# Storing a transposed gradient by column groups, loading it in four transfers, and another order of the last four rows

## The chip, the cores and the metric

The kernel runs on one core of a Trainium2 chip. The core has a tensor engine (PE, with its weight loads shown apart as PEld), a vector engine (DVE), a scalar engine (ACT), GpSimd (POOL) and a sync engine (SP). Transfers are carried by 16 DMA engines, which SP, ACT and POOL feed through queues of their own. The metric is the time of one execution on the device in microseconds, the median of several runs.

## The reference

The program computes the forward pass and all gradients of a block for 2048 tokens of width 640: a linear attention with 32 heads of width 20, and a gated feed-forward part of width 1728.

```
h  = x + attention(layernorm(x))          # phi(q) (phi(k)^T v) / (phi(q) z), then @ wo
g, u = n2 @ w_gate, n2 @ w_up             # n2 = layernorm(h)
h2 = h + (silu(g) * u) @ w_down
outputs: h2, and the gradients of x, wqkv, wo, w_gate, w_up, w_down for a given grad_out
```

What matters here is one step of the backward pass. Let dd be the gradients by g and u, side by side: 2048 tokens by 3456 columns. The gradient that enters the second layernorm is dd times the transpose of (w_gate, w_up), so PE needs dd transposed, with columns on partitions. The gradient dh1 at h is the backward of that layernorm plus grad_out. From dh1 the attention's gradients follow: dp = dh1 times W2 transposed (W2 joins wo and the key-value matrices), sums of dp by head, dq, and GT = dh1^T times the scaled phi(q).

## The kernel before

**Tiles.** 2048 tokens are 16 rows of 128 (row t holds tokens 128t to 128t+127). The columns of the feed-forward part are taken in four groups of 448, 448, 448 and 384 (`GW`). One group of dd, g and u together, gives 7, 7, 7 and 6 tiles of 128 columns (`GK`), 27 in all (`NKT`).

**The feed-forward backward pass (L784 to L892).** For each group g, row pairs are computed: PE forms g and u, ACT applies sigmoids and copies, DVE makes dd. Each row of dd is then transposed by a DMA on SP into a stage tile `stg` (three buffers, L829), and stored from there by SP into the DRAM scratch `scr_dT` (`store_dT`, L780 to L782), one store behind the transposition. `scr_dT` has, for each row and partition, all 27 tiles side by side: 6912 bytes, of which a store writes 1792 or 1536. Behind the rows of a group, `dw_group` (L668 on) makes the group's weight gradients. It uses PSUM banks in turn; there are four. ACT and DVE copy results out and so free the banks.

**The dh loop (L1058 to L1143).** Eight steps p take two rows each, 2p and 2p+1. `load_cols(p)` (L167) brings the transposed dd of both rows back from `scr_dT` in one transfer of 1728 KB, into a strip `cols`. The product is done by a scheme with seven half-size products, so DVE first makes sums of quarters of `cols` (`col_sum`, L661). The loads of steps 0 and 1 are issued by ACT (`act_load`, L158), at the head of dw_group's ACT work in the last group and at its end; those of steps 2 to 7 by POOL (`pool_load`, L161) in step p for step p+2 (L1113). Behind the product comes the layernorm's backward: `ln_sum`, `ln_dot`, `ln_b` and `ln_c`. `ln_c` (L971) lets POOL issue a DMA that adds the result to dh1 (in the trace `dh<-lb_a`, L974), and SP one that transposes the row of dh1 (`dh1T<-dh`, L977). `dp_mm(t)` (L984) multiplies it, some rows later: in step p rows 2p-5 and 2p-4. `dp_a` takes the sums by head (L994 to L997), `widen` (L1002, on ACT) spreads them over the columns, and `dp_b` (L1004 to L1014) makes dq.

**WO pieces.** Five DMA transpositions of wo (`tr_piece`, L907) are spread over the steps by `WO_AT` (L947).

**Behind the loop (L1144 to L1199).** Rows 11 to 15 still need dp, sums and dq. `dp_1` is dp_a with both widenings, `dp_2` is dp_b and the load of a later row of phi(q) (`load_q`). PE fills in with GT blocks (`gt_part`, L923): blocks 0, 1 and 2 over rows 0 to 11 first, each holding a PSUM bank, so that one bank is left for dp. `xn_act` (L1016, ACT) turns rows of x into normalized ones. After it, SP issues 16 transpositions of wqkv (`wqkvT`), and POOL loads `xnT_r`, in their own order.

**What sets the order.** In these stages PE, DVE, ACT, SP and POOL follow the order of the source, each for itself. The built program counts the landings of DMAs on semaphores in rotation, eight for those of SP and ACT together and eight for those of POOL; a DMA is issued only when the earlier one on its semaphore has landed. The issuing engine does this wait, in its order.

Of the kernel before, what the change touches and what calls it, by code (L numbers as in the profile page):

```python
# [9 lines left out]
BF16 = mybir.dt.bfloat16  # L10
# [5 lines left out]
P = 128  # L16
# [4 lines left out]
def kernel(  # L21
# [8 lines left out]
    nc = tc.nc  # L30
    _, S, D = A_x.shape
    F = B_w_gate.shape[1]
    Dh = D // H
    ST = S // P
# [6 lines left out]
    GK = [7, 7, 7, 6]  # L41
    KO = [0, 7, 14, 21]
    NKT = 27
# [13 lines left out]
    dram = ctx.enter_context(tc.tile_pool(name="dram", bufs=1, space=bass.MemoryType.DRAM))  # L57
    psum = ctx.enter_context(tc.tile_pool(name="psum", bufs=4, space=bass.MemoryType.PSUM))
    big = ctx.enter_context(tc.tile_pool(name="big", bufs=5))
    strips = ctx.enter_context(tc.tile_pool(name="strips", bufs=4))  # L60
    small = ctx.enter_context(tc.tile_pool(name="small", bufs=4))

    def mm(name):

        return psum.tile([P, 2, 512], FP32, name=name, tag="mm")
# [4 lines left out]
    def half(ap):  # L70
        return ap.rearrange("p (c n) -> p c n", c=2)
# [3 lines left out]
    def wk(name, w=D, pool=0):  # L75
        return wpools[pool].tile([P, w], BF16, name=name, tag="w", padded_shape=[P, D])

    def dram_tm(name, W):
        t = dram.tile([S, W], BF16, name=name)
        return t, t.rearrange("(t p) w -> p t w", p=P)  # L80
# [4 lines left out]
    scr_pqs, scr_pqs_v = dram_tm("scr_pqs", D)  # L85
    scr_h1, scr_h1_v = dram_tm("scr_h1", D)
    scr_m, scr_m_v = dram_tm("scr_m", FT * P)
    scr_dT = dram.tile([ST, P, NKT, P], BF16, name="scr_dT")
    scr_dm, scr_dm_v = dram_tm("scr_dm", GW[3])
    scr_dwdT = dram.tile([D, FT * P], BF16, name="scr_dwdT")  # L90
    scr_Yt = dram.tile([D, D], BF16, name="scr_Yt")
# [64 lines left out]
    colp = {}  # L156
# [7 lines left out]
    def pool_store(out, in_):  # L164
        tc.keep_in_program_order(nc.gpsimd.dma_start(out=out, in_=in_))

    def load_cols(p, load=pool_load):  # L167
        colp[p] = strips.tile([P, 2, NKT, P], BF16, name="cols", tag="S")
        load(colp[p][:], scr_dT[2 * p:2 * p + 2].rearrange("t p k c -> p t k c"))

    def stage():
        return small.tile([P, 7, P], BF16, name="stg", tag="stg", bufs=3)
# [446 lines left out]
    with tc.manual_schedule(engines={EngineType.SP}):  # L619
# [159 lines left out]

        def store_dT(g):  # L780
            t, stg = staged.pop(0)
            nc.sync.dma_start(out=scr_dT[t, :, KO[g]:KO[g] + GK[g], :], in_=stg[:, :GK[g], :])  # L782

        for g in range(4):  # L784
            w = GW[g]
# [3 lines left out]
            for t in range(0, ST, 2):  # L789
# [37 lines left out]
                for c in range(2):  # L827
                    stg = stage()
# [4 lines left out]
                if g == 2 and 2 <= t <= 2 * NE:  # L833
                    i = t // 2 - 1
# [77 lines left out]
    gts = {}  # L912
# [4 lines left out]
    def pqs_of(t):  # L917
        return pqs_t[0][:, t, :] if t < NA else pqs_t[1][:, t - NA, :]
# [4 lines left out]
    def gt_part(ps, i, t0, t1, by=ST):  # L923
        for ci, (n0, n1), t in [(ci, n, t) for a in range(t0, t1, by) for ci, n in enumerate(NCH)
                                for t in range(a, min(a + by, t1))]:
                nc.tensor.matmul(ps[:, ci, :320], lhsT=dh1[:, t, i * P:(i + 1) * P], rhs=pqs_of(t)[:, n0:n1],
                                 start=(t == 0), stop=(t == ST - 1))

    with tc.manual_schedule(engines={EngineType.PE, EngineType.DVE, EngineType.Activation, EngineType.SP, EngineType.Pool}):
# [14 lines left out]
        s1, u2, u3 = (kept[:, i * 320:(i + 1) * 320] for i in range(3))  # L944
        sub = dict(op=ALU.subtract)
        NPR = ST // 2
        WO_AT = {0: (0, 1), 1: (2,), 6: (3,), 7: (4,)}  # L947
        X, Y, lb, dps, pqs, dh1Ts, dwds = {}, {}, {}, {}, {}, {}, {}

        def prod(out, p, lhs, rhs, first=False, left=None):  # L950
# [33 lines left out]
        def dp_mm(t):  # L984
            if t >= 0:
                x = dh1Ts.pop(t)
                dps[t] = wk("dp")
                ps = mm("ps_dp")
                mm_row(ps, lambda i: x[:, i, :], lambda i, n0, n1: W2T[:, i, n0:n1], DT)
                nc.scalar.copy(out=half(dps[t][:]), in_=row(ps))  # L990
# [25 lines left out]
        def xn_act(ts):  # L1016
            for t in ts:
                nc.scalar.activation(out=hn[:, t, :], in_=hn[:, t, :], func=ACT.Identity, scale=rstd1[:, t:t + 1],
                                     bias=nmr1[:, t:t + 1])
# [5 lines left out]
        def store_dwd(p):  # L1025
            if p >= 0:
                r0 = (NE + p) * P
                nc.gpsimd.dma_start(out=out_6[r0:min(r0 + P, F), :], in_=dwds.pop(p)[:min(P, F - r0), :])
# [29 lines left out]
        for p in range(NPR):  # L1058


            q1, q2 = 2 * p - 1, 2 * p - 2
            f, h = 2 * p - 5, 2 * p - 4
            if p > 0:
                ln_sum(q2, dy2)
                ln_dot(q2, dy2)
            if p == 0:
                pq_load(range(13, ST), False, nc.gpsimd.dma_start)
            load_q(h)
            if p not in (1, 2):
                p1(p)  # L1070
            Y[p] = mm("ps_dhc")
            A, C, Dd = X[p][:, 0, :320], Y[p][:, 0, :320], Y[p][:, 1, :320]
            prod(Dd, p, col_blk(p, 0, 1), B21, first=True, left=(0, BL[:, 0:320]))
            widen(rx, rall, h - 2)
            dp_a(h - 2)
            col_sum(p, 2)
            if p > 0:
                ln_b(q2)
            widen(pr, nS1, h - 2)
            if p >= NPR - 3:  # L1080
                xn_act(range(2 * (p - NPR + 3), 2 * (p - NPR + 3) + 2))
            if p > 0:
                p3(p - 1)
                if p == NPR - 2:
                    pqs_t[0] = strips.tile([P, NA, D], BF16, name="pqs_a", tag="S")
                    pqs_load(0, 3)
                    pqs_load(3, 6)
                elif p == NPR - 1:
                    pqs_load(6, NA)
                ln_c(q2, dy2)  # L1090
            dp_b(h - 2)
            load_q(2 * p - 3)
            if p > 0:
                c12(p - 1)
                if p == 1:
                    pq_norm(range(13, ST), nc.gpsimd.dma_start)
            else:
                nc.vector.tensor_tensor(out=T5, in0=BL[:, 0:320], in1=BL[:, 320:D], **sub)
                nc.vector.tensor_tensor(out=T4, in0=B21, in1=T2, **sub)
                nc.vector.scalar_tensor_tensor(out=nmr1[:], in0=mv1[:, :, 0], scalar=-1.0, in1=rstd1[:],  # L1100
                                               op0=ALU.mult, op1=ALU.mult)
            for x in (p5, p6) if f >= 0 else (p6, p5):
                x(p)
            if p == NPR - 1:
                pqs_t[1] = big.tile([P, ST, D], BF16, name="pqs_b", tag="B")
                pqs_load(NA, ST)
            if p > 0:
                ln_sum(q1, dy1[(p - 1) % 2])
                ln_dot(q1, dy1[(p - 1) % 2])
            comb(dy1[p % 2][:, 0:320], Dd, p, 0, s1)  # L1110
            col_sum(p, 4)
            if p + 2 < NPR:
                load_cols(p + 2)  # L1113
            dp_mm(f)
            if p > 0:
                ln_b(q1)
            prod(A, p, col_blk(p, 1, 0), T3, left=(1, BL[:, 320:D]))
            scaled(u3, A, p, 1)
            widen(rx, rall, f)
            dp_a(f)  # L1120
            widen(pr, nS1, f)
            comb(dy2[:, 320:D], C, p, 1, u3)
            if p > 0:
                ln_c(q1, dy1[(p - 1) % 2])
            dp_mm(h)
            store_dwd(p - 2)
            if p < NPR - 1:
                tr_dwd(p)
            if p + 1 < NPR:
                col_sum(p + 1, 1)  # L1130
            dp_b(f)
            if p + 1 < NPR:
                col_sum(p + 1, 3)
            if p < 2:
                p1(p + 1)
            prod(A, p, col_blk(p, 1, 1), T4, left=(1, T5))
            scaled(dy2[:, 0:320], A, p, 1)
            for i in WO_AT.get(p, ()):
                tr_piece(woT, A_wo, i)
            if p in (3, 5, 6):  # L1140
                t = 4 * (p // 2) - 4 if p < 6 else 8
                (nc.gpsimd if p < 6 else nc.sync).dma_start(out=hn[:, t:t + 4, :], in_=x_v[:, t:t + 4, :])
        p = NPR - 1  # L1143
# [21 lines left out]
        def dp_1(t):  # L1165
            dp_a(t, prs[t % 2])
            widen(rxs[t % 2], rall, t)
            widen(prs[t % 2], nS1, t)

        def dp_2(t):  # L1170
            last = dp_b(t, prs[t % 2], rxs[t % 2])
            return last, load_q(t + 3)
# [2 lines left out]
        dp_mm(ST - 4)  # L1175
        dp_1(ST - 4)
        dp_2(ST - 5)
        last_pq = dp_2(ST - 4)[1]
        nc.gpsimd.dma_start(out=hn[:, ST - 4:ST, :], in_=x_v[:, ST - 4:ST, :])
        store_dwd(p - 1)  # L1180
        store_dwd(p)
        xn_act(range(6, 8))
        for i, t in ((0, None), (1, ST - 3), (2, ST - 2)):
            gts[i] = mm("ps_gt")
            gt_part(gts[i], i, 0, ST - 4, ST if i else 4)
            if t:
                dp_mm(t)
                dp_1(t)
                xn_act(range(t - 5, t - 3) if t == ST - 3 else range(t - 4, t - 3))
        GT = mat(2 * DT * D, DT, D)  # L1190
        ps = gts.pop(0)
        gt_part(ps, 0, ST - 4, ST)
        nc.scalar.copy(out=half(GT[:, 0, :]), in_=row(ps))
        dp_2(ST - 3)
        dp_mm(ST - 1)
        dp_1(ST - 1)
        dp_2(ST - 2)
        xn_act(range(11, ST - 4))
# [2 lines left out]
    with tc.manual_schedule(engines={EngineType.SP, EngineType.DVE}):  # L1201
# [41 lines left out]
        for ci, (n0, n1) in enumerate(NCH):  # L1243
            for t in range(ST):
                c = 32 * (t % 4)
# [244 lines left out]
        with tc.manual_schedule(engines={EngineType.PE, EngineType.Activation}):  # L1490
# [21 lines left out]
            for p in range(NP):  # L1512
# [32 lines left out]
                if p not in (2, 3):  # L1545
                    f, i = small_q.pop(0)
# [64 lines left out]
```

## Time and profile before

| | us |
|---|---|
| median of 3 runs | 790.19 (790.06 to 790.34) |
| the profiled execution | 795.75 |
| its span, from the first to the last instruction | 794.0 |
| PE busy | 778.3 |
| DVE busy | 576.2 |
| ACT busy | 331.7 |
| dh loop, from its first matmul to the last product | 437 to 559 |
| rows behind it, until the last GT matmul | 559 to 592 |

The granted clock of PE was 0.999 of full speed. All times in the text are us from the start of the span. Lines of a timeline give start, duration, engine, source line, operation and tiles (`out<-in`), then in brackets how long the engine was idle before and what ended that. Lines of waits give total, number and longest. DMA lines give the number, the size and the median time from issue to landing. The lines of the chain of work give start, duration and what ran. A matmul of 320 columns is listed with 299 ns, but one follows the other every 136 ns, since they are pipelined.

### The profile page before, as it was taken

To read this page: it belongs to the slowest core of one execution; us is meant where nothing else is said; L and a number is where in the kernel's file an instruction comes from. 1 tells how busy PE (TensorE), PEld (TensorE's weight loads), DVE (VectorE), ACT (ScalarE), POOL (GpSimd) and SP (SyncE) were. 2 spreads that over 40 slices of the span, in tenths; PEclk is the share of its full clock that TensorE was granted. 3 is DMA by queue.
4 is the path that set the end of the run, shared out by engine and by line. 5 is a ranking of instruction groups with operands and counts; after the bars stand their busy time and mean duration, and the time that the engine had idled before them with its cause. 6 is when DMAs were issued, how large, how long until landed. Compare 5 with 4: busy or idle time off the path is not lost.

```text
span 794.0 us, 13716 instructions
## 1 busy us (share of the span) xinstructions
PE 778.3 (98%) x5243; PEld 496.6 (63%) x5243; DVE 576.2 (73%) x1005; ACT 331.7 (42%) x490; POOL 208.7 (26%) x357
## 2 busy tenths in 40 slices
PE   9999999999999999999999998999979999999997
PEld 7676566555555555555666776677757777777665
DVE  7989988894697648848988668899862366626672
ACT  6962532760283045402831245567652233323001
POOL 4600047413301111134133232231531111113220
PEclk9999999999999999999999999999999999999999
DMA  9899999999979988999898899997899878999992
GB/s 261 164 240 310 195 226 255 242 272 224 246 189 231 203 184 200 252 247 201 202 231 206 288 205 218 183 259 202 171 237 198 152 152 171 167 239 228 194 266 84
DMA packets 293043, 170.62 MB, mean 215 GB/s; under 512 B 242396, under 2 KB 280925, under 8 KB 292976
## 3 DMA queue, kind: packets, MB, share of 16 engines
q1 hardware_dynamic: 271552, 102.84, 66.3%
q0 software_dynamic: 18528, 61.57, 28.3%
q10 hardware_dynamic: 2896, 5.33, 2.2%
q8 instruction: 41, 0.67, 0.4%
q14 instruction: 26, 0.21, 0.1%
HBM read 52.92 MB, written 56.28 MB: 138 GB/s over the span
## 4 chain that ended last, share of the span: by engine, by line
PE 85%; DMA 6%; DVE 4%; issue 2%; SPq 2%; ACT 1%; POOL 1%; DVEq 0%; ACTq 0%; POOLq 0%
PE ps_dw L878 10%; PE ps_dxn L1356 8%; PE pu L798 7%; PE ps_wa L687 7%; PE pg L793 7%; PE ps_dwqk L1275 6%; PE ps_dm L420 5%; PE ps_dhn L952 4%; PE ps_kq L308 4%; PE ps_dhc L952 3%; PE ps_wc L687 3%; PE ps_dk L110 3%; PE ps_y L511 3%; PE ps_a L574 3%; PE ps_oa L1426 2%
## 5 line engine op out<-in xcount | busy, mean ns | idle before, releaser
L952 PEld LDWEIGHTS <-cols 128*128 128x128 bf16 x624 | 61.1, 98 | 23.8
L798 PE MATMUL pu<-wgu,hnT 128*128 128x448 bf16 (+1 forms) x320 | 63.6, 346 | 0.0
L793 PE MATMUL pg<-wgu,hnT 128*128 128x448 bf16 (+1 forms) x320 | 63.6, 346 | 0.0
L878 PE MATMUL ps_dw<-m_s,dh 128*128 128x448 bf16 (+1 forms) x320 | 60.4, 346 | 0.0
L1356 PEld LDWEIGHTS <-ring 128*128 128x128 bf16 x480 | 47.0, 98 | 18.2
L1356 PE MATMUL ps_dxn<-wqkvT,ring 128*128 128x320 bf16 x320 | 51.3, 299 | 0.0
L798 PEld LDWEIGHTS <-hnT 128*128 128x128 bf16 x320 | 31.3, 98 | 27.1
L878 PEld LDWEIGHTS <-dh 128*128 128x128 bf16 x320 | 31.3, 98 | 27.1
L793 PEld LDWEIGHTS <-hnT 128*128 128x128 bf16 x320 | 31.3, 98 | 27.0
L420 PEld LDWEIGHTS <-dh2T 128*128 128x128 bf16 x320 | 31.0, 98 | 25.1
L420 PE MATMUL ps_dm<-wdT,dh2T 128*128 128x448 bf16 (+1 forms) x240 | 46.5, 344 | 0.0
L814 ACT ACTIVATE dd<-pg 128x896 bf16<-128x896 f32 (+1 forms) x32 | 28.5, 891 | 40.4 <-PE pg L793 40.4
L308 PE MATMUL ps_kq<-wqk,xnT 128*128 128x320 bf16 x320 | 44.9, 299 | 0.4 <-DMA xnT<-xn 0.3
L308 PEld LDWEIGHTS <-xnT 128*128 128x128 bf16 x320 | 30.8, 98 | 12.8 <-DMA xnT<-xn 0.6
L687 PEld LDWEIGHTS <-S 128*128 128x128 bf16 x256 | 25.1, 98 | 21.7
L1275 PEld LDWEIGHTS <-hn 128*128 128x128 bf16 x320 | 31.0, 98 | 12.2 <-issue 0.3
L140 POOL TENSOR_SCALAR lnv<-mv 128x1 f32<-128x1 f32 x32 | 12.0, 374 | 89.6 <-DVE mv L136 73.5
L148 DVE CUSTOM_DVE_ANT_0 lb_a<-lb_dy,hn 128x640 bf16<-128x640 bf16 x16 | 13.2, 826 | 30.4 <-ACT lb_dy L146 30.4
L840 POOL DMA_DIRECT2D scr_m<-m_s x16 | 12.1, 759 | 86.8 <-DVE m_s L826 86.8
L683 DVE TENSOR_TENSOR dd<-dd 128x3584 bf16<-128x3584 bf16 (+1 forms) x12 | 23.1, 1954 | 15.5 <-DMA scr_dT<-stg 7.8
L974 POOL DMA_DIRECT2D dh<-lb_a x16 | 14.4, 900 | 73.4 <-DVE lb_a L973 67.7
L146 ACT ACTIVATE lb_dy<-ps_dxn,rstd 128x640 bf16<-128x640 f32 x16 | 12.7, 794 | 45.0 <-PE ps_dxn L1356 45.0
(259 smaller groups left out, 1775.4 us busy)
## 6 DMA issues: line engine op xcount, KB each, us to landing
scr_dT<-stg SPq DMA_DIRECT2D x48, 224.0 KB, 3.0
cols<-scr_dT POOLq DMA_DIRECT2D x6, 1728.0 KB, 11.4
scr_m<-m_s POOLq DMA_DIRECT2D x12, 448.0 KB, 4.7
pq<-scr_pq POOLq DMA_DIRECT2D x32, 160.0 KB, 6.0
cols<-scr_dT ACTq DMA_DIRECT2D x2, 1728.0 KB, 10.2
hn<-in_A_x_dram SPq DMA_DIRECT2D x5, 640.0 KB, 5.1
scr_dT<-stg SPq DMA_DIRECT2D x16, 192.0 KB, 2.5
scr_pq<-pqa SPq DMA_DIRECT2D x4, 640.0 KB, 4.3
```

What stands on the lines that cost most here:

```text
L110: nc.tensor.matmul(ps[:, ci, :320], lhsT=lhs(k), rhs=rhs(k, *NCH[ci]), start=(start and k == 0), stop=(stop and k == n - 1))
L308: nc.tensor.matmul(ps[:, ci, :320], lhsT=xnT[:, t, k, :], rhs=wqk[:, k, w0 + n0:w0 + n1], start=(k == 0), stop=(k == DT - 1))
L420: nc.tensor.matmul(ps[:, c, :w], lhsT=dh2T[:, kt, (t + c) * P:(t + c + 1) * P], rhs=wdT[:, kt, o:o + w], start=(kt == 0), stop=(kt == DT - 1))
L511: nc.tensor.matmul(ps[:, ci, :320], lhsT=xn[:, t, i * P:(i + 1) * P], rhs=pk[:, t, n0:n1], start=(t == 0), stop=(t == ST - 1))
L687: nc.tensor.matmul(out, lhsT=lhs[:, t, :], rhs=rhs[:, t, :], start=(first and t == 0), stop=(t == 7), skip_group_check=not first)
L793: nc.tensor.matmul(pg[:, c, :w], lhsT=hnT[:, kt, (t + c) * P:(t + c + 1) * P], rhs=wg[:, kt, 0:w], start=(kt == 0), stop=(kt == DT - 1))
L798: nc.tensor.matmul(pu[:, c, :w], lhsT=hnT[:, kt, (t + c) * P:(t + c + 1) * P], rhs=wg[:, kt, w:2 * w], start=(kt == 0), stop=(kt == DT - 1))
L814: sig = nc.scalar.activation(out=dg, in_=pg[:, :, :w], func=ACT.Sigmoid)
L878: nc.tensor.matmul(ps[:, c, :w], lhsT=lhs(t), rhs=rhs(t), start=(t == 0), stop=(t == ST - 1))
L952: nc.tensor.matmul(out, lhsT=lhs[:, k, :], rhs=rhs[:, k, :], start=(first and k == 0), stop=(k == HKG - 1), skip_group_check=not first)
L1275: nc.tensor.matmul(ps[:, ci, :320], lhsT=xn_r[:, t, i * P:(i + 1) * P], rhs=dq[t // 8][:, t % 8, n0:n1] if which == 0 else dk[:, t, n0:n1] ...
L1356: nc.tensor.matmul(ps[:, ci, :320], lhsT=lhs[:, i, :], rhs=rhs[:, i, n0:n1], start=(k == 0 and i == 0), stop=(k == 2 and i == DT - 1))
```

## The change

It has three parts.

- `scr_dT` is laid out by column group first. A store then writes whole rows of its group's block. `load_cols` takes a list of groups and issues one transfer for each: rows of 1792 bytes (1536 in the last group) in place of 6912. The steps on ACT issue all four at once. In the loop, groups 0 and 1 are issued where the whole load was, and groups 2 and 3 behind `ln_c` of the odd row.
- WO piece 2 moves from step 1 to step 0.
- Behind the loop, row 13's sums come ahead of row 12's second half, and so on for rows 13 to 15, and the `xn_act` rows are placed behind row 14's and row 15's copies.

```diff
-    scr_dT = dram.tile([ST, P, NKT, P], BF16, name="scr_dT")
+    scr_dT = dram.tile([4, ST, P, 7, P], BF16, name="scr_dT")
...
-    def load_cols(p, load=pool_load):
-        colp[p] = strips.tile([P, 2, NKT, P], BF16, name="cols", tag="S")
-        load(colp[p][:], scr_dT[2 * p:2 * p + 2].rearrange("t p k c -> p t k c"))
+    def load_cols(p, load=pool_load, gs=range(4)):
+        if gs[0] == 0:
+            colp[p] = strips.tile([P, 2, NKT, P], BF16, name="cols", tag="S")
+        for g in gs:
+            load(colp[p][:, :, KO[g]:KO[g] + GK[g], :],
+                 scr_dT[g, 2 * p:2 * p + 2, :, :GK[g], :].rearrange("t p k c -> p t k c"))
...
-            nc.sync.dma_start(out=scr_dT[t, :, KO[g]:KO[g] + GK[g], :], in_=stg[:, :GK[g], :])
+            nc.sync.dma_start(out=scr_dT[g, t, :, :GK[g], :], in_=stg[:, :GK[g], :])
...
-        WO_AT = {0: (0, 1), 1: (2,), 6: (3,), 7: (4,)}
+        WO_AT = {0: (0, 1, 2), 6: (3,), 7: (4,)}
...
             if p + 2 < NPR:
-                load_cols(p + 2)
+                load_cols(p + 2, gs=(0, 1))
...
             dp_mm(h)
+            if p + 2 < NPR:
+                load_cols(p + 2, gs=(2, 3))
             store_dwd(p - 2)
...
         dp_mm(ST - 4)
         dp_1(ST - 4)
         dp_2(ST - 5)
+        for i in (0, 1):
+            gts[i] = mm("ps_gt")
+            gt_part(gts[i], i, 0, ST - 4, ST if i else 4)
+        dp_mm(ST - 3)
+        dp_1(ST - 3)
         last_pq = dp_2(ST - 4)[1]
         nc.gpsimd.dma_start(out=hn[:, ST - 4:ST, :], in_=x_v[:, ST - 4:ST, :])
         store_dwd(p - 1)
         store_dwd(p)
-        xn_act(range(6, 8))
-        for i, t in ((0, None), (1, ST - 3), (2, ST - 2)):
-            gts[i] = mm("ps_gt")
-            gt_part(gts[i], i, 0, ST - 4, ST if i else 4)
-            if t:
-                dp_mm(t)
-                dp_1(t)
-                xn_act(range(t - 5, t - 3) if t == ST - 3 else range(t - 4, t - 3))
+        gts[2] = mm("ps_gt")
+        gt_part(gts[2], 2, 0, ST - 4)
+        dp_mm(ST - 2)
+        xn_act(range(6, 9))
+        dp_1(ST - 2)
+        dp_2(ST - 3)
         GT = mat(2 * DT * D, DT, D)
         ps = gts.pop(0)
         gt_part(ps, 0, ST - 4, ST)
         nc.scalar.copy(out=half(GT[:, 0, :]), in_=row(ps))
-        dp_2(ST - 3)
         dp_mm(ST - 1)
+        xn_act(range(9, 11))
         dp_1(ST - 1)
         dp_2(ST - 2)
         xn_act(range(11, ST - 4))
```

## The prediction

> **What bounds the kernel now.** I read the page first: its head and the busy times.
>
> ```profile
> span 794.0 us, 13716 instructions
> PE 778.3 (98%) x5243; PEld 496.6 (63%) x5243; DVE 576.2 (73%) x1005; ACT 331.7 (42%) x490; POOL 208.7 (26%) x357
> ```
>
> TensorE is busy for all but 15.7 us of 794.0, and the change leaves the number and shapes of its matmuls alone. So the change can only shorten or lengthen waits of PE. The waits view for PE alone between 430 and 600 us, the stretch of the dh loop and the rows behind it, gives the whole stock:
>
> ```profile
> PE ps_dp L110 <- ACT dp L990: 3.5, 1, 3.5
> PE ps_dp L110 <- DVE wsum L666: 2.5, 1, 2.5
> PE ps_dp L110 <- DMA dh1T<-dh: 1.2, 1, 1.2
> PE ps_gt L926 <- ACT mats L1193: 0.8, 1, 0.8
> ```
>
> Columns: total us, times, longest. Two of these (2.5 + 1.2 = 3.7 us) lie in the loop, two (4.3 us) behind it. The 2.5 is misnamed: the matmul starts at 490.14, and the transposed row 2 (dh1T) landed at 490.10. The second loop wait, row 3, is in the chain of work that ended last:
>
> ```profile
> 473.89 13.61 DMA dh<-lb_a
> 487.51 16.32 DMA dh1T<-dh
> 503.88 1.53 PE ps_dp L110 x10
> ```
>
> The accumulate into dh took 13.6 us and its transposition 16.3 us, and the matmul followed at once. The accumulate stood on POOL's queue behind a 1728 KB cols load issued at 467.17 and landed at 482.02.
>
> Behind the loop, the ACT timeline shows why PE waits 3.5 us:
>
> ```profile
> 572.87 0.72 ACT L1002 CAST dq<-rall 128x640 bf16<-128x640 f32 x1
> 576.57 0.72 ACT L1002 COPY dzb<-nS 128x640 bf16<-128x640 bf16 x1 [2.98 <-DVE nS L997]
> 577.20 1.73 ACT L1018 ACTIVATE hn<-hn,nmr,rstd 128x640 bf16<-128x640 bf16 x2
> 578.83 0.67 ACT L990 CAST dp<-ps_dp 128x640 bf16<-128x640 f32 x1
> ```
>
> ACT waits for row 13's sums, which DVE makes only after finishing rows 11 and 12; then two xn operations; then the copy that frees row 14's PSUM bank for row 15 (PE resumes at 579.55).
>
> I also looked before the loop, because load_cols(0) and (1) are issued on ACT. ACT timeline, then PE timeline:
>
> ```profile
> 401.21 0.83 ACT L820 CAST u<-pu 128x768 bf16<-128x768 f32 x1
> 410.75 0.37 ACTq L159 DMA_DIRECT2D cols<-scr_dT  x1
> 411.21 0.80 ACT L880 CAST dwev<-ps_dw 128x768 bf16<-128x768 f32 x1 [9.17 <-DMA scr_dT<-stg]
> ```
>
> ```profile
> 416.16 2.76 PE L878 MATMUL ps_dw<-m_s,dh 128*128 128x384 bf16 x16
> 418.76 2.76 PE L687 MATMUL ps_wc<-dd,S 128*128 128x384 bf16 x16
> ```
>
> ACT stood 9.2 us with the load at its head. It costs nothing: L880's copy frees the bank of ps_wc, which starts only at 418.76.
>
> **What the Trainium skill says.** "DMA: Bandwidth & Descriptors", section on the anatomy of one DMA (SWDGE path): the DMA engines wait on no semaphore, a wait happens on the issuing sequencer before dispatch. The trace agrees: ACT's 9.2 us. Same page, "Queues, rings and completion order": each engine takes turns between its queues, a packet at a time. That makes a cols packet what a transposition waits for. In the packet records a 6912-byte packet takes 262 ns at the median, a 256-byte packet of a transposition 18, and the 1792-byte packets of the scr_dT stores 74. But the turns alone would not give 16 us (40 packets per engine), so the trace agrees only in direction.
>
> **The change part by part.**
>
> *Stores in the new layout.* 64 stores, each row still 1792 or 1536 bytes: 0.
>
> *Rows of the loads.* Four packets in place of one: 3 x 74 + 65 (1536 bytes) = 287 ns against 262, 10% more transfer time, on queues that PE doesn't wait for directly. POOL issues four DMAs for one, three times about 0.55 us extra a step; POOL waits 3 to 8 us for DVE in every step, so 0.
>
> *Loads around the dh1 transfer.* Half the bytes now stand ahead of the odd row's accumulate, half behind it, so it should land some 4 to 7 us earlier; row 2's transposition also loses the WO piece that stood ahead of it in SP's queue (8.9 us at the head of that queue). Both loop waits should go: gain up to 3.7. What is late next: rows 4, 5 and 6 landed only 1.7, 1.8 and 1.1 us ahead of use, so if their transfers don't move, the gain stops at 1.1. The later half of a load is issued up to 9 us later; cols of steps 4 and 6 landed 7.1 and 6.7 us ahead of their sums, and the whole load takes 7.6 to 17 us, so a loss is possible: -1 to +3.7. I take +2.0.
>
> *WO piece 2 in step 0.* One more transposition (1.3 us of SP issue) at 448, where SP has nothing waiting until 457: 0.
>
> *Rows 12 to 15.* New order on DVE: sums of row 13 before the second half of row 12, and so on; on ACT: row 14's copy ahead of xn. Using the durations above: DVE ends row 11 at 572.7; sums of row 13 (0.52 + 0.85 + 0.2) until 574.25; ACT widens until 574.9, copies row 14 until 575.5; PE has the bank when its 8 GT matmuls end at 575.5: the 3.5 us are gone. ACT: three xn until 578.0, two widens until 579.3 (row 14's sums are ready at 577.95; its pq landed at 576.01), GT copy until 579.9. PE, through its 26 matmuls at 579.05, waits 0.85 there as it waited 0.76 before: the fourth GT block (i = 3) starts at 579.95, before it was 583.59. Gain 3.6. The later GT copies now stand behind rows 14 and 15 on ACT, but end at about 584.9, and ps_dz needs the bank at 588.65. Row 15's pq is issued 1.5 us later (576.3), lands at about 581, needed at 580.6. SP's 16 wqkvT transpositions don't move with it; the first dk row they delay landed at 619.85 for 624.27, 4.4 us of slack for 3.6.
>
> *The four ACT loads.* The cost I find is here. The built program counts landings of SP's and ACT's DMAs on eight semaphores in turn, and a DMA waits until its predecessor on that semaphore has landed. The old load waited for row 10's transposition (410.57). The four new ones wait for that, and for the stores of rows 10, 11 and 12. In the profile of before these landed at 421.07, 423.38 and 424.84:
>
> ```profile
> scr_dT<-stg SPq DMA_DIRECT2D x1, 192.0 KB, 10.5
> scr_dT<-stg SPq DMA_DIRECT2D x1, 192.0 KB, 8.1
> scr_dT<-stg SPq DMA_DIRECT2D x1, 192.0 KB, 1.9
> ```
>
> (DMA issues in the moments 410.59, 415.27 and 422.94; last column us to landing.) All of ACT's work stands behind: L880's copy (bank of ps_wc, 418.76) and the two s1 copies, which DVE needs before its own copy of ps_dw, whose bank PE needs at 421.36. From ACT's release, 0.7 (L880) + 0.9 (s1 twice) + 0.5 + 1.1 + 0.5 (DVE: last sum, wsum, copy) = 3.7 us to that bank: ACT free later than 417.6 costs PE one for one. How late? Upper end: store of row 12 as in before, 424.84 + 0.4 = 425.3, cost 425.3 + 3.7 - 421.4 = 7.6. Lower end: the stores land by 417, cost 0, since the old load (11.5 us, 410.75 to 422.28) shared the engines with them. In group 1, without such a load, the time from row 10's transposition (250.90) to row 12's store (261.97) was 11.1 us; from 410.57 this gives 421.7; a short-row load takes less from them than the old one, so I take ACT free at 421: cost 3.3. The load of step 1 (434.7) waits for DMAs landed by 428 and adds 3 x 0.37 us of issue ahead of an operation due at 438.98: 0.
>
> *Sum.* -3.6 - 2.0 + 3.3 = -2.3 on the profiled span: 794.0 to 791.7. The profiled execution took 795.75, 5.6 above the median 790.19; the waits are taken to be the same in both, so 790.2 - 2.3 = 787.9.
>
> **Rivals.**
> 1. *ACT is not held long.* The stores land by 417: no cost. -3.6 - 2.0 to -3.7: 783 to 785. For: the old load is gone from their path. Against: group 1's 11.1 us.
> 2. *Slower: the ACT queue decides.* Row 12's store lands no earlier than before, ACT is free at 425.3, PE loses 7.6; with no loop gain, +7.6 - 3.6 = +4.0: 794.2. It decides from ACT being free at about 423 (5.6 against 3.6 + 2.0). For: the chain store, load, store through the stage buffers is serial, with POOL's stores beside it. Against: row 12 was 9.6 us in transposition under the old load.
> 3. *Gains hidden.* Rows 4 to 6 come late in place of 2 and 3 (loop 0), or the dk rows behind SP's queue take back 1 to 2 us: -3.6 + 3.3 + 0 to 1.5: 790 to 791.5. For: slack of 1.1 to 1.8 and 4.4 us. Against: their accumulates move with PE.
>
> **How the numbers follow.** Forecast 0.44 (own range 786 to 789.5), first rival 0.19, second 0.18, third 0.19. A measurement of this kernel tells 0.2%, 1.6 us, from no change: faster is below 788.6, slower above 791.8. Faster: 0.37 of the forecast's 0.44, the first rival's 0.19, 0.02 of the third: 0.58. Same: 0.07 + 0.17 = 0.24. Slower: 0.18. The range, 783 to 793, leaves out most of rival two and the end of rival one.
>
> **What would show it.** The PE waits of 3.5, 2.5 and 1.2 us gone, the GT wait near 0.8 kept; the accumulates of odd rows landing in under 8 us; dh1T ahead of ps_dp in every row. On ACT, four loads between 411 and 421 and a PE wait of about 3 us at ps_wc or ps_dw near 419, not there before. The forecast is wrong if ACT is free before 417 or after 424, or if a ps_dp wait stays in the loop.

## The result

| | us |
|---|---|
| before, median of 6 | 790.53 (790.06 to 804.44) |
| after, median of 6 | 803.89 (796.57 to 812.33) |
| ratio, 95% interval | 1.0144 (1.0099 to 1.0190) |
| a later comparison (e6 below), 20 executions of after | 802.60, ratio 1.0087 (1.0056 to 1.0118) |

The change makes the kernel slower. The forecast was 787.9, its range ended at 793. Over all chips used here single executions of the kernel before ran from 789.6 to 819.3 us, more than its first three times had shown, and the ratios leave out those that stand far above the fastest.

The profiled execution of after took 812.33, the longest of the six. Its page, the head and the busy times:

```profile
span 810.6 us, 13753 instructions
PE 785.4 (97%) x5243; PEld 499.4 (62%) x5243; DVE 575.8 (71%) x1005; ACT 331.5 (41%) x490; POOL 221.2 (27%) x375
```

TensorE has the same 5243 matmuls, but is busy 7.1 us longer, so some of them ran slower. The waits of PE over the whole span (total us, times, longest):

```profile
PE ps_wc L690 <- ACT dwev L883: 7.6, 1, 7.6
PE ps_oa L1434 <- DVE h1r L1418: 4.8, 2, 3.9
PE ps_dxn L1364 <- DMA wvk<-wvk: 4.0, 1, 4.0
PE ps_dxn L1364 <- DMA ring<-dk: 1.9, 1, 1.9
PE ps_gt L929 <- ACT mats L1201: 1.2, 1, 1.2
```

All three waits at ps_dp that before had are gone (3.5, 2.5 and 1.2). The largest new one is 7.6 us at ps_wc, for ACT. ACT's timeline of after (start, duration, engine, line; in brackets the idle time ahead of it):

```profile
410.97 14.94 ACTq L159 DMA_DIRECT2D cols<-scr_dT  x4
426.01 0.80 ACT L883 CAST dwev<-ps_dw 128x768 bf16<-128x768 f32 x1 [23.59 <-DMA stg<-dd]
```

and PE's timeline of the same stretch:

```profile
416.53 2.76 PE L881 MATMUL ps_dw<-m_s,dh 128*128 128x384 bf16 x16
426.86 5.28 PE L690 MATMUL ps_wc<-dd,S 128*128 128x384 bf16 x16 [7.56 <-ACT dwev L883]
431.93 5.59 PE L881 MATMUL ps_dw<-m_s,dh 128*128 128x384 bf16 x32
```

In before ACT's copy came at 411.21. Now four loads hold ACT until 425.9. The bracket names a transposition, but the transfer records show what each load waited for: the second, third and fourth went out at 419.13, 420.17 and 425.54, each 0.02 us after the store of row 10, 11 or 12 had landed (419.11, 420.15, 425.52). These three stores (DMA issues in the moments 410.89, 415.52 and 420.38; last column us to landing):

```profile
scr_dT<-stg SPq DMA_DIRECT2D x1, 192.0 KB, 8.2
scr_dT<-stg SPq DMA_DIRECT2D x1, 192.0 KB, 4.6
scr_dT<-stg SPq DMA_DIRECT2D x1, 192.0 KB, 5.1
```

The 16 matmuls of ps_wc then took 5.28 us where before had 2.76. Busy time by stretches of 2 us for after (PE, PEld, DVE, ACT and POOL, each with its number of instructions); the number ahead of the last two is the clock granted to PE:

```profile
418.00:420.00 2.00, 1.30 (x8) 0.68 (x7) 0.00 (x0) 0.00 (x0) 0.00 (x0) 1.00 0.47 132
...
422.00:424.00 2.00, 0.00 (x0) 0.00 (x0) 0.00 (x0) 0.00 (x0) 0.00 (x0) 0.54 1.13 309
...
428.00:430.00 2.00, 2.00 (x7) 0.88 (x6) 2.00 (x4) 0.00 (x0) 0.00 (x0) 0.50 1.13 347
...
432.00:434.00 2.00, 2.00 (x13) 1.16 (x12) 1.83 (x2) 0.00 (x0) 1.73 (x4) 0.90 0.50 128
```

PE ran at half clock from 422.2 to 432.4: 7 matmuls in 2 us in place of 14. The hold cost 7.6 us of waiting and about 2.8 more of slow matmuls. The first matmul of the dh loop starts at 447.76; before had it at 436.96.

To follow the rest, I cut every profile at five matmuls: the first ps_dhn (start of the loop), the first of the last row of 13 ps_dhc (its end), the first ps_dz, the first ps_dxn, and the first ps_dk behind that. The last column is the rest of the span. The runs marked with e are told below; e5 is the kernel before and e6 the kernel after, profiled once more. All in us.

| | loop starts | loop | rows 12 to 15 and GT | first ps_dxn, to the next ps_dk | rest |
|---|---|---|---|---|---|
| before | 437.0 | 120.3 | 35.1 | 4.1 | 165.7 |
| e5, before again | 437.1 | 116.3 | 36.9 | 4.1 | 163.5 |
| after | 447.8 | 116.3 | 32.1 | 12.8 | 169.8 |
| e6, after again | 448.0 | 116.3 | 31.5 | 4.1 | 165.0 |

(31.9 us between ps_dz and the first ps_dxn are the same in all four.) Against e5, the kernel after loses 10.7 to 10.9 us ahead of the loop, gains nothing in it, gains 4.8 to 5.4 behind it, and in one of two executions loses another 8.7 where ps_dxn waits for wvk and ring.

### The profile page after: what moved, and what is told of

It is laid out like the page before. It is cut to its first block, busy times and chain, and to the rows that moved or that the text cites. A ratio compares the mean times of both kernels' runs of the same rounds, so it can differ in the third digit from the quotient of the medians.

```text
span 810.6 us, 13753 instructions
## 1 busy us (share of the span) xinstructions
PE 785.4 (97%) x5243; PEld 499.4 (62%) x5243; DVE 575.8 (71%) x1005; ACT 331.5 (41%) x490; POOL 221.2 (27%) x375
## 4 chain that ended last, share of the span: by engine, by line
PE 80%; DMA 5%; issue 5%; DVE 5%; SPq 2%; POOL 2%; ACT 1%; POOLq 0%; ACTq 0%; DVEq 0%
PE ps_dw L881 9%; PE ps_dxn L1364 8%; PE ps_wa L690 7%; PE pg L796 6%; PE pu L801 6%; PE ps_dwqk L1283 5%; PE ps_dm L423 5%; PE ps_dhn L955 5%; PE ps_dhc L955 4%; PE ps_kq L311 4%; PE ps_wc L690 3%; PE ps_y L514 3%; PE ps_a L577 3%; PE ps_dk L110 3%; PE ps_oa L1434 2%
## 5 line engine op out<-in xcount | busy, mean ns | idle before, releaser
L1364 PE MATMUL ps_dxn<-wqkvT,ring 128*128 128x320 bf16 x320 | 53.1, 306 | 1.9 <-DMA ring<-dk 1.9
L881 PEld LDWEIGHTS <-dh 128*128 128x128 bf16 x320 | 31.5, 98 | 27.4 <-issue 0.5
L817 ACT ACTIVATE dd<-pg 128x896 bf16<-128x896 f32 (+1 forms) x32 | 28.5, 890 | 40.4 <-PE pg L796 40.4
L690 PEld LDWEIGHTS <-S 128*128 128x128 bf16 x256 | 25.7, 101 | 30.9 <-issue 10.2
L311 PEld LDWEIGHTS <-xnT 128*128 128x128 bf16 x320 | 30.9, 98 | 12.8 <-DMA xnT<-xn 0.8
L690 PE MATMUL ps_wc<-dd,S 128*128 128x448 bf16 (+1 forms) x128 | 27.2, 370 | 7.6 <-ACT dwev L883 7.6
L1372 POOL DMA_DIRECT2D out_dram<-dx x16 | 8.7, 544 | 89.0 <-DVE pkr L1332 64.9
## 6 DMA issues: line engine op xcount, KB each, us to landing
cols<-scr_dT POOLq DMA_DIRECT2D x18, 448.0 KB, 5.2
scr_m<-m_s POOLq DMA_DIRECT2D x12, 448.0 KB, 4.5
cols<-scr_dT ACTq DMA_DIRECT2D x6, 448.0 KB, 4.8
```

The source lines that it names most:

```text
L311: nc.tensor.matmul(ps[:, ci, :320], lhsT=xnT[:, t, k, :], rhs=wqk[:, k, w0 + n0:w0 + n1], start=(k == 0), stop=(k == DT - 1))
L690: nc.tensor.matmul(out, lhsT=lhs[:, t, :], rhs=rhs[:, t, :], start=(first and t == 0), stop=(t == 7), skip_group_check=not first)
L817: sig = nc.scalar.activation(out=dg, in_=pg[:, :, :w], func=ACT.Sigmoid)
L881: nc.tensor.matmul(ps[:, c, :w], lhsT=lhs(t), rhs=rhs(t), start=(t == 0), stop=(t == ST - 1))
L1364: nc.tensor.matmul(ps[:, ci, :320], lhsT=lhs[:, i, :], rhs=rhs[:, i, n0:n1], start=(k == 0 and i == 0), stop=(k == 2 and i == DT - 1))
```

## The experiments

Each run has its own 2 to 20 executions and executions of before on the same chip; ratios are to these, with 95% intervals. On one chip each ran e1 to e4, e5 to e8, e9 to e11, e12 to e15, e16 with e17, and e18.

### Taking the hold and the tail apart (e1 to e4)

e1 is the kernel after, but step 0's loads stand behind ACT's two s1 copies in dw_group:

```diff
             store(ev, 0, 0)
+            if g == 3:
+                load_cols(0, act_load)
...
-                load_cols(0, act_load)
```

> The changed kernel, but step 0's four loads are issued by ACT behind its two s1 copies of the last group, not ahead of all of them. Theory: the 7.6 us wait of ps_wc for ACT and the half clock behind it (16 matmuls in 5.28 us in place of 2.76) come from ACT being held by the loads; both go, 10 to 11 us less than the changed kernel (about 802), so 790 to 793. What is left above 784 is then the wait for wvk in the stage of ps_dxn and the half clock behind it (some 8.7 us). Rival: the loads themselves come too late for the first sums of step 0, whoever issues them; then a wait of PE at the first ps_dhn takes the place and the time stays above 798.

e2 is the kernel before with the diff's lines behind the loop and nothing else.

> The kernel before with the other order of rows 12 to 15 and nothing else. Theory: ps_dp's wait of 3.5 us goes, but POOL's loads behind the last row of phi(q) are issued some 8 us later and run into SP's transpositions of wqkv; a wait of PE of 3 to 6 us at ps_dxn for wvk or ring appears, with half clock behind it: 793 to 798. Rival: the late wvk came from the shifted loop of the changed kernel and not from the order; then 786 to 788.

e3 is e1 with the lines behind the loop taken back to those of before; e4 is after with these lines taken back.

> The new layout, the split loads around the dh1 transfer and WO piece 2 in step 0, with step 0's loads behind the s1 copies and the rows 12 to 15 in the order of the kernel before. Theory: the loop's two waits (2.5 and 1.2 us) are gone, ps_dp's wait of 3.5 stays, no wait at wvk: 786 to 787. Rival (the loads' new rows or their queue also delay the stage behind): 790 or more.

> The changed kernel with the rows 12 to 15 in the order of the kernel before. Theory: hold of ACT with its half clock +10.8, loop -4.0: 796 to 798, with no wait at wvk. Rival (the wvk wait follows from the delay of the loop): 802 to 805.

| | median us | ratio to before | loop starts | loop | rows 12 to 15 and GT | ps_dxn to ps_dk |
|---|---|---|---|---|---|---|
| e1 | 792.30 | 0.9972 (0.9910 to 1.0035) | 437.1 | 116.3 | 31.5 | 12.3 |
| e2 | 791.47 | 0.9986 (0.9916 to 1.0056) | 437.5 | 116.3 | 31.5 | 10.5 |
| e3 | 802.17 | 1.0111 (1.0061 to 1.0162) | 441.5 | 116.3 | 36.8 | 7.8 |
| e4 | 805.77 | 1.0147 (1.0074 to 1.0220) | 444.8 | 116.3 | 37.0 | 8.9 |

The hold is settled. With the loads behind the copies (e1) the wait at ps_wc is gone and the loop starts where it did before; no wait at ps_dhn takes its place. With the loads at the head (e4) ps_wc waits 5.6 us and the loop starts 7.8 us later than in e5. (e3's later start is another thing: 2.7 us at ps_wc of an earlier group, at 193, for DVE, with 3.4 us at half clock behind it.)

The order behind the loop is settled too: 31.5 with it, 36.8 to 37.0 without.

Two expectations fell. The loop takes 116.3 in e2, whose loads are those of before: the 3.7 us of waits that the profile of before shows there are not the usual case. And the late wvk or ring is not tied to the tail's order: e3 and e4, with the order of before, lose 3.7 and 4.8 us there, e1 and e2, with the new order, 8.2 and 6.4.

### Is the profile of before typical, and is it POOL? (e5 to e8)

e5 and e6 are before and after unchanged.

> The kernel before once more, for a second profile of it. The theory now: the two waits of the dh loop (2.5 and 1.2 us) belong to the one profiled execution (795.75) and not to the kernel: the loop from the first ps_dhn to the last ps_dhc takes 116.3 us here, as in every other trace, in place of 120.3, and the stage behind it 36.8 in place of 35.1. Rival: the waits stand again and the loop takes 120.

> The changed kernel once more, on the same chip as the others. Theory: ACT is held beyond 423 by its four loads again, ps_wc waits 5 to 8 us and runs its next 5 us at half clock, the loop takes 116.3, the rows behind it 31.5 to 32.1, and the stage of ps_dxn loses 6 to 9 us for wvk and ring: 796 to 805. Rival: the hold was one execution's: 790 to 793.

e7 is e1 with POOL's lines moved up, so that the load of x, two stores and the loads of xnT_r go out behind row 14's load of phi(q):

```diff
-        dp_2(ST - 5)
+        last_pq = dp_2(ST - 5)[1]
+        nc.gpsimd.dma_start(out=hn[:, ST - 4:ST, :], in_=x_v[:, ST - 4:ST, :])
+        store_dwd(p - 1)
+        store_dwd(p)
...
-        last_pq = dp_2(ST - 4)[1]
-        nc.gpsimd.dma_start(out=hn[:, ST - 4:ST, :], in_=x_v[:, ST - 4:ST, :])
-        store_dwd(p - 1)
-        store_dwd(p)
+        dp_2(ST - 4)
```

> The changed kernel with step 0's loads behind the s1 copies, and with POOL's load of the last rows of x, its two stores and the loads of xnT_r behind the last but one row of phi(q), some 8 us earlier, so that they are over before SP's transpositions of wqkv are needed. Theory: what makes wvk late at ps_dxn is this burst of POOL's; the 8 us lost there shrink to below 4: 783 to 788. Rival (SP's queue is late because PE is early, whatever POOL does): 790 to 793, the waits for wvk and ring as in the run with the loads behind.

e8 is e2 with the same edit.

> The kernel before with the other order of rows 12 to 15 and the same earlier burst; loads, layout and WO pieces as before. Theory (the loop gains nothing from the new loads): the same time as the kernel above with the new loads, within 2 us: 783 to 788. Rival (the new layout and the split help, or hurt): 4 us or more apart.

Medians of 20: e5 793.19, e6 802.60, e7 796.32 (ratio 0.9989, 0.9955 to 1.0022), e8 798.49 (0.9974, 0.9935 to 1.0013); before had 795.22 on this chip. Neither e7 nor e8 came near the 783 to 788 expected.

e5 answers the first question. Its whole list of PE waits above 1 us between 430 and 600:

```profile
PE ps_dp L110 <- ACT dp L990: 3.5, 1, 3.5
```

No wait in the loop, and the span is 789.7 in place of 794.0. The wait behind the loop is there, and dearer than in the first profile of before. PE's timeline of e5:

```profile
575.60 2.82 PE L110 MATMUL ps_dp<-mats,dh1T 128*128 128x320 bf16 x10 [3.49 <-ACT dp L990]
578.22 3.40 PE L926 MATMUL ps_gt<-pqs_b,dh 128*128 128x320 bf16 x13
```

Ten matmuls took 2.82 us; in before's profile, after a wait of 3.51, they took 1.52. Here PE was at half clock from 574.4 to 581.2. So removing this wait is worth 5.4 us (36.9 to 31.5) where so much half clock follows it, and 3.6 where none does, as in the first profile of before (35.1).

e6 shows the hold a second time. Its PE waits between 400 and 600:

```profile
PE ps_wc L690 <- ACT dwev L883: 6.9, 1, 6.9
PE ps_gt L929 <- ACT mats L1201: 0.6, 1, 0.6
```

e7 and e8 have no wait at ps_dxn (4.1 us in both), but PE also comes there later, because they lose as much ahead of it (e8 waits 5.5 us at ps_dz). PE waits of e7:

```profile
PE ps_dz L1255 <- ACT mats L1245: 7.9, 1, 7.9
```

Row 15's load of phi(q), issued at 573.33, now took 16.3 us among POOL's loads (3.5 in after), so row 15's sums, the GT copies behind them on ACT and ps_dz came late. So POOL's loads must not stand ahead of that row. Where else they may stand is e12's and e18's question.

### The number of loads or their layout? A smaller tail? (e9 to e11)

e9 is the kernel before with step 0's load cut into four, in the old layout:

```diff
-        load(colp[p][:], scr_dT[2 * p:2 * p + 2].rearrange("t p k c -> p t k c"))
+        for a, n in zip(KO, GK) if p == 0 else ((0, NKT),):
+            load(colp[p][:, :, a:a + n, :], scr_dT[2 * p:2 * p + 2, :, a:a + n, :].rearrange("t p k c -> p t k c"))
```

> The kernel before, with step 0's load alone cut into four (layout with 27 tiles side by side, all other loads and the rows 12 to 15 as before). Theory: what holds ACT is the number of its loads, since each waits for a landing of SP's, the last for the store of row 12. ACT's first copy behind them starts after 423 again, ps_wc waits 5 to 8 us, the first ps_dhn comes 8 to 11 us later than in the kernel before: 799 to 805. Rival (the new layout delays the stores for which ACT waits): no wait above 2 us at ps_wc, 791 to 796.

e10 is the kernel before with row 14's copy ahead of row 13's widenings on ACT:

```diff
             if t:
                 dp_mm(t)
-                dp_1(t)
-                xn_act(range(t - 5, t - 3) if t == ST - 3 else range(t - 4, t - 3))
+        for t in (ST - 3, ST - 2):
+            dp_1(t)
+            xn_act(range(t - 5, t - 3) if t == ST - 3 else range(t - 4, t - 3))
```

> The kernel before, with one thing changed on ACT: the copy of row 14's dp stands ahead of the widenings of row 13 and of the xn rows. The order on DVE and POOL stays. Theory: the wait of 3.5 us of ps_dp goes with the half clock that follows it in some executions (4 to 5 us in sum), the last row of phi(q) and POOL's loads stay early: 786 to 789. Rival (the time is bound by SP's transpositions in the stage of ps_dxn, so that an earlier PE waits there): 791 to 794, with a wait for wvk or ring of 3 us or more.

e11 is e1 again.

> The changed kernel with step 0's loads behind the s1 copies, once more, beside the run above. Theory: no hold of ACT, loop 116.3 us, rows behind it 31.5; the median lies 3 to 6 us below the kernel before if the stage of ps_dxn runs free, and level with it if it waits for wvk or ring.

e10: 795.26, ratio 1.0012 (0.9984 to 1.0039). The 3.5 us at ps_dp went, 2.4 came at ps_gt (rows 12 to 15 and GT took 33.1), and the median did not move. e11: 794.08, ratio 1.0010 (0.9976 to 1.0043): loop 116.3, rows behind it 31.5, and 11.6 from ps_dxn to ps_dk, as in e1. Without the hold the change is neither faster nor slower.

e9: 821.24, ratio 1.0323 (1.0273 to 1.0373), far beyond what I expected. PE waits of e9 between 400 and 600:

```profile
PE ps_dp L110 <- DMA dh1T<-dh: 14.7, 1, 14.7
PE ps_wc L688 <- ACT dwev L881: 8.5, 1, 8.5
```

The hold is there in the old layout, so it comes from four loads in place of one. But a second wait, 14.7 us for a transposed row of dh1, stands in the loop, which takes 133.0. The kernel after has the same hold and no such wait. So some part of the change does protect the loop.

### Which part keeps the loop free? (e14 to e17)

All four have the hold of four ACT loads and the tail of before. e14 is e9 with WO piece 2 in step 0. e15 has the new layout and its short rows, all four loads at once where the whole load was, and the WO piece in step 1. e16 adds to e15 the split around the dh1 transfer; e17 adds to e15 the WO piece in step 0. e4 has all three.

> The kernel before with step 0's load cut into four in the old layout, and WO piece 2 in step 0. If the WO piece at the head of SP's queue makes row 2's dh1T late, the wait of 14.7 us in the loop goes and the time falls to 799 to 805; if the long rows of the loop's loads do, it stays at 812 to 822.

> The changed kernel with ACT's hold, WO piece 2 in step 1, all four loads of a step issued at once where the whole load was, and rows 12 to 15 in the order of the kernel before: of the change only the layout and the short rows. If the short rows keep the loop free, no wait for dh1T and 800 to 806; if the split around the dh1 transfer or the WO piece does it, a wait of 5 us or more in the loop and 808 to 822.

> The changed kernel with ACT's hold, WO piece 2 in step 1 and rows 12 to 15 in the order of the kernel before: short rows and the split around the dh1 transfer. If the split frees the loop, no wait for dh1T, first ps_dhn to last ps_dhc 116.3 us, 800 to 806. If it needs the WO piece moved, a wait of 3 us or more for dh1T, 806 to 818.

> As the run beside it, but with WO piece 2 in step 0 and all four loads of a step at once: short rows and the WO piece, no split. If the WO piece is what frees the loop, with short rows it takes 116.3 and the time is 800 to 806; if the split is needed, a wait for dh1T of some 6 us stays, as with the old loads: 804 to 812.

| | rows | split | WO piece 2 | loop, us | wait for dh1T | median us |
|---|---|---|---|---|---|---|
| e9 | long | no | step 1 | 133.0 | 14.7 | 821.24 |
| e14 | long | no | step 0 | 123.9 | 6.1 | 805.12 |
| e15 | short | no | step 1 | 133.0 | 15.0 | 816.70 |
| e17 | short | no | step 0 | 120.5 | 2.7 | 814.45 |
| e16 | short | yes | step 1 | 116.3 | none | 809.51 |
| e4 | short | yes | step 0 | 116.3 | none | 805.77 |

The loop column is the one to read: the medians come from four chips, those of e14 to e17 from two executions each (e17's profiled one took 821.8). Short rows alone do nothing. The split frees the loop without the WO piece: PE waits of e16 between 400 and 600:

```profile
PE ps_wc L690 <- ACT dwev L883: 7.2, 1, 7.2
PE ps_dp L110 <- ACT dp L993: 3.5, 1, 3.5
```

The WO piece alone does half or more, 9.1 us of 16.7 in e14 and 12.5 in e17. Each row stands on one profile; with the split, after and e6 have 116.3 too. In e9 SP's timeline shows why it matters:

```profile
477.27 1.23 SPq L978 DMA_TRANSPOSE dh1T<-dh  x1
478.55 2.06 SPq L1024 DMA_TRANSPOSE dwd<-scr_dwdT  x1
480.67 10.58 SPq L909 DMA_TRANSPOSE mats<-in_A_wo_dram  x1
491.35 8.61 SPq L978 DMA_TRANSPOSE dh1T<-dh  x2
```

The WO piece stood 10.6 us at the head of SP's queue. Row 2's transposition went out behind it at 491.35 and took 21.2 us beside a cols load of 1728 KB. With the split (e16) the transpositions of the same rows took 6 to 11 us.

### What wvk and ring wait for, and a better version (e12, e13, e18)

e12 is e1, but of the four loads of xnT_r (rows 0 to 3, 4 to 7 and so on) only the first stays where it was:

```diff
-        for c in range(4):
-          with tc.issue_after(last_pq):
-            pool_load(xnT_r[:, 4 * c:4 * c + 4], scr_xnT[4 * c:4 * c + 4].rearrange("t p k c -> p t k c"))
+        def load_xnT(c, load=pool_store):
+            load(xnT_r[:, 4 * c:4 * c + 4], scr_xnT[4 * c:4 * c + 4].rearrange("t p k c -> p t k c"))
+
+        with tc.issue_after(last_pq):
+            load_xnT(0, pool_load)
...
         for t in range(ST + LAG):
...
+            if t in (0, 2, 5):
+                load_xnT({0: 1, 2: 2, 5: 3}[t])
```

> The changed kernel with step 0's loads behind the s1 copies, and of the four loads of xnT_r only the first where it was; the others (rows 4 to 15) are issued in the stage of ps_dk, some two rows ahead of use. 1.9 MB less then stand beside SP's transpositions of wqkv. Theory (POOL's burst makes wvk and ring late): both waits at ps_dxn go, the 5.4 us stay: 784 to 788. Rival (SP's own queue of 16 transpositions is what is late): the waits stay within 1.5 us of the run with the loads behind, 790 to 794.

e13 is e2 with the same edit.

> The kernel before with the other order of rows 12 to 15 and the same loads of xnT_r put off; all loads of cols, the layout and the WO pieces as before. Theory: in the usual execution the new loads gain nothing in the loop, so this stands within 2 us of the kernel above; but more of its executions have a wait for dh1T in the loop, so that its times spread further upward. Rival: the new loads gain or lose 3 us or more in every execution.

e12: median of 20 788.39, ratio 0.9929 (0.9896 to 0.9961). e13: 789.99, ratio 0.9961 (0.9933 to 0.9990). They are the first versions clearly faster than before, e12 by 0.7%. e13, which has none of the new loads, is within 1.6 us of e12, so the loads around the dh1 transfer show no gain here. 11 of e12's executions lie between 785.5 and 789.1. But its profile, of an execution of 794.37, shows the waits still: 2.1 at wvk, 3.9 at ring; e13's has 4.5 at ps_dxn. In e12 the second load of xnT_r went out at 604.83, and the transpositions of wvk issued from 606.57 on took 8 to 11 us. So e18 (on another chip) leaves the first two loads early; the edit against e12:

```diff
         with tc.issue_after(last_pq):
             load_xnT(0, pool_load)
+            load_xnT(1, pool_load)
...
-            if t in (0, 2, 5):
-                load_xnT({0: 1, 2: 2, 5: 3}[t])
+            if t in (4, 8):
+                load_xnT(1 + t // 4)
```

> The changed kernel with step 0's loads behind the s1 copies, the first two loads of xnT_r where they were, the last two in the stage of ps_dxn, four rows ahead of use. Theory: the transpositions of wvk meet no load of 640 KB any more, no wait at ps_dxn above 1 us, 784 to 788 in most executions, median at or below the run with three loads put off (0.993 of the kernel before). Rival (SP's own queue is late): waits of 3 us or more stay in the profile and half of the executions lie above 790.

e18: 791.22, ratio 0.9966 (0.9940 to 0.9993). Its profile spans 788.1 us. Its PE waits:

```profile
PE ps_oa L1440 <- DVE h1r L1424: 2.2, 1, 2.2
PE ps_warm L347 <- DVE ones L249: 1.1, 1, 1.1
PE ps_dwv L129 <- ACT dwv L1393: 0.8, 1, 0.8
PE ps_gt L930 <- ACT mats L1202: 0.6, 1, 0.6
```

No wait at ps_dxn. Loop 116.3, rows behind it 31.5, ps_dxn to ps_dk 4.1: in this execution the 5.4 us of the new order are still there at ps_dk. Of these, 3.6 go again in the last stage (rest 167.1 against 163.5 in e5), with the 2.2 us of waiting for h1r and half clock behind it. The expectation was missed: 13 of the 20 executions lie above 790, and the ratio is not below that of e12. One profile without the wait proves little, since e5 and e6 have none either.

Over all profiles the length of SP's transpositions says more. SP's timelines of after and then of e18 (start, us until the last of the ten has gone out; 26.99 in e6):

```profile
587.49 35.90 SPq L911 DMA_TRANSPOSE wqkvT<-in_A_wqkv_dram  x10
```

```profile
575.00 22.47 SPq L912 DMA_TRANSPOSE wqkvT<-in_A_wqkv_dram  x10
```

wvk and ring stand behind these in SP's order. In the 17 profiles with all four loads of xnT_r ahead of them, the longest of the 16 transpositions of wqkv took 18.8 to 28.5 us. Where it took 22.5 or more (ten profiles), PE lost 3.4 to 8.7 us in the stage of ps_dxn; where it took 21.8 or less (seven), 0.3 at most. With one or two loads there (e12, e13, e18) it took 13.3 to 18.0; in e12 and e13 a load put off then met wvk, whose transpositions took up to 10.9 and 9.4. So with fewer of POOL's loads of 640 KB beside them SP's transpositions were faster, and where they were slow wvk and ring came late. That nothing else makes them late is not shown. Not settled either is why one execution has the wait and another not: in after the four loads took 16.7 to 18.2 us each, in e6, the same kernel, 9.7 to 11.4. Nor did I follow the wait for h1r in the last stage (0 to 4.8 us), which comes and goes in kernels of both kinds.

## Why the prediction was wrong

**The hold of ACT: right mechanism, wrong size.** The prediction found the four loads, the stores that they wait for and the bank that PE lacks. The failed term is "I take ACT free at 421". It rested on the 11.1 us from row 10's transposition to row 12's store in group 1, and on the thought that short loads leave the stores more room. Measured: the three stores took 8.2, 4.6 and 5.1 us and the last landed at 425.52; ACT copied at 426.01. The upper end, which the prediction had worked out (425.3), was the right value. The short loads left room for the first two stores (10.5 and 8.1 in before), but since each load goes out when a store lands, they then stood beside row 12's (1.9 in before). In group 1 neither a cols load nor the last group's additional POOL stores (issued from 406.4 to 410.1) stood beside the chain; which of the two made the difference was not tested.

**"ACT free later than 417.6 costs PE one for one".** This failed too. It costs 7.6 us of waiting, as the prediction's upper end had it, plus the half clock behind: 10.7 us ahead of the loop in after (10.9 in e6). The Trainium skill states a cause in "TensorE: Matmul & The Clock Gate", section "Part 1: The HAM clock gate": an idle window of about 3.4 us brings PE to half clock, and the windows run freely. The traces agree in part. Half clock came in stretches of 3.4, 6.8, 10.2 and 13.7 us, and equal gaps had unequal effects, as if it mattered where in a window they fall. But a window need not be idle throughout: in e12 and e18 gaps of 2.1 and 2.2 us brought half clock. The prediction did not price it.

**The loop: a gain of 2.0 was booked, none was to be had.** The step that failed is "the waits are taken to be the same in both". The profiled execution of before took 795.75 where the median was 790.2, and the loop waits were a part of that difference: 120.3 us there, 116.3 in e5. The mechanism was sound. e15 and e16, which differ in the split alone, show it worth 16.7 us, when the loop starts 10 us later and runs into such a wait.

**The tail: right mechanism, undersized.** The 3.5 us at ps_dp went and the GT wait stayed (0.6 to 1.2; 0.85 was predicted). The gain was 4.8 to 5.4 in place of 3.6, because this wait brought half clock with it in seven of the nine profiles that have it. Against the profile of before, where it did not, the predicted 3.6 came out (35.1 to 31.5 in e6).

**The stage of ps_dxn.** "4.4 us of slack for 3.6" is the failed step of rival three, which priced it at 1 to 2. SP's transpositions took up to 26.5 us each where before had up to 19.4, and the stage lost 8.7 in after and 6.4 to 8.2 in e1, e2 and e11, though nothing in e6, where they took up to 18.8. The prediction moved POOL's row 15 load by 1.5 us, but not the nine loads and stores behind it on POOL: in after they began 8.2 us later than in before, and the PE work that they must not delay only 3.8 us later.

**Zero-cost edits.** The stores, POOL's additional issues (busy 221.2 in place of 208.7), the loads of step 1 and the WO piece made no wait of PE. These steps held.

**Rivals.** Rival two was the right one, with its place and its 425.3. Its 794.2 lacked the half clock. With measured terms, 790.2 + 10.9 - 5.4 gives 795.7. The stage of ps_dxn and the last stage added 15.0 in after and 1.5 in e6 (against e5), so the median of 802 to 804 lies between; how often they add how much is open. Rival two had a chance of 0.18, and the range cut most of it off.

## What to carry to other kernels

Cutting one transfer into four on an engine that also computes can add waits on that engine: find the last transfer that each must wait for, and take the end of the chain that a profile shows rather than a hoped one. A wait of PE above 2 us is priced with the half clock that may follow it, in gains as in costs. Where the profiled execution is longer than the median, its waits are suspects: a part of them is the difference, and a second profile tells which.

## What the runs showed of the hardware

- Idle stretches of PE between 2.1 and 3.6 us may or may not bring half clock: 2.1 and 2.2 us did in e12 and e18, and at the same ps_dp wait of 3.5 us, e5 had 6.8 us of it and before none.
- A DMA transposition of one row of dh1 (160 KB) took 2.6 us at the least. Beside a cols load of 1728 KB it took up to 21 in before and e9 and 24 in e14, but 9 at most in e5; beside the same bytes in four loads 21 in e17 and 32 in e15. Rows of 1792 bytes in place of 6912 did not help (loop 133.0 in e9 and e15); issuing half of the load behind the odd row's transfer did (116.3 in e16).
